# A planned order, fixed buffer places, cosines by absolute values and 128-lane convolution pairs in a two-branch sequence mixer

## The chip, the cores and the metric

The kernel runs on one core of a Trainium2 chip. The core has a matrix engine (PE, whose weight loads the profile lists apart as PEld), three engines for elementwise work (DVE, ACT, POOL), a queue engine (SP) and 16 DMA engines that all queues share. Each engine works through its own list of instructions in order and waits on semaphores where one needs what another engine or a DMA makes. The metric is the device time in microseconds of one execution; lower is better.

## The reference, cut to what matters

The input is `u`, 2048 positions by 640 channels. Two branches are mixed by a gate per position.

```python
g = _sigmoid((x * gate_w).sum(-1, keepdims=True))
# a: a long convolution per channel with a kernel of 128 damped oscillations
P = jnp.exp((A * dt[:, None])[:, :, None] * pos[None, None, :])
K = 2.0 * jnp.einsum("dn,dnl->dl", C, P).real
y = jnp.fft.irfft(jnp.fft.rfft(u_t, 2*L) * jnp.fft.rfft(K, 2*L), 2*L)[:, :, :L]   # + u * D_skip
# b: a filter in the two-dimensional spectrum
X = jnp.fft.rfft2(x) * (w_r + 1j * w_i)
b = jnp.fft.irfft2(X, s=(S, D))
return g * a + (1 - g) * b
```

Nothing of this changes.

## The kernel before, in words

The work is in five stages, with letters used from here on. Channels are cut into four chunks of 160, c = 0 to 3.

- **P** (`phase_p`): small vectors of the parameters, split into three bfloat16 parts each and written to DRAM.
- **A** (`phase_a`, first half): the first two steps of the length-4096 transform of `u`, as matrix products in float32. `stage1` (L353) multiplies blocks of 64 by 128, `stage2` (L366) blocks of 64 by 160; ACT or DVE copies each result out of PSUM (L400) and the result `u_d` goes to DRAM. Beside it the gate's sums (L435).
- **F** (`phase_a`, second half): the two-dimensional spectrum in nine groups of rows: transposes (L533), products (L487, L492), the filter on DVE (L563 to L573), the way back (L583 to L599); result `s3e_d` in DRAM.
- **K** (`phase_b`): the convolution kernel, 40 steps t in batches of five. Per step `mags` makes exponentials (L686, ACT L688), `outer` and `inner` make a phase product each (L696) and one ACT sine over 1024 columns each (L703, L715) that gives sine and cosine at once; POOL multiplies one factor (L706), DVE the other (L718, L719, L720), and PE combines them (L735) into `k_d` in DRAM.
- **C** (`phase_c`, `phase_d`): per chunk, the kernel's transform (L353, L366), the product with `u_d` on DVE (L830, L831), the sum and difference of its halves (L835, L836), the product back (L849), a copy (L851) and a write to `s3_d`; later the last step reads `s3e_d` into `t3e` (L889) and `s3_d` into `t3` (L901, each load writing every fourth lane), multiplies (L170, L928), applies the gate (L911, L931 to L934) and writes out.

Each buffer is a tile from a pool, with its own entry in the bookkeeping of waits. The order is written by generators that are merged by weights: A, then F, then the first transform of C run as one stream beside the stream of P and K (`merge((194.0, ga), (76.8, gl))`); C follows when both are done. DMAs are issued from SP, ACT and POOL.

Of the kernel before, what the change touches and what calls it, by code (L numbers as in the profile page):

```python
# [11 lines left out]
I32 = mybir.dt.int32  # L12
# [11 lines left out]
NP = 33  # L24
MAGIC = 12582912.0
# [3 lines left out]

# [13 lines left out]
def _tables():  # L51
# [34 lines left out]
    w3 = np.swapaxes(w2, 1, 2) * wk[:, None, None]  # L86
    w2[K0, 64:] = 0.0
# [28 lines left out]
    rx, ry, rm = np.zeros((128, 2, 16, 32)), np.zeros((128, 2, 8, 2, 32)), np.zeros((128, 8, 96))  # L116
    rx[[51, 115], 1] = ry[[57, 121], 1] = 1.0
    ry = ry.swapaxes(2, 3)
    for x in range(16):
        r = 64 * (x // 8) + 6 * (x % 8)  # L120
        rm[r:r + 3, x % 8, 0:64] = A_ORDER
        rm[r:r + 3, x % 8, 64:96] = 64 * j
        rm[r + 3:r + 6, x % 8, 64:96] = 1.0
        r = 3 * x if x < 10 else 3 * x + 2
        for h in (0, 64):
            rx[h + r:h + r + 3, 0, x] = j + 0.5
        rx[94 if x < 10 else 114, 0, x] = 1.0
# [39 lines left out]
def halved(nc, out, w, x):  # L167

    for i in (0, 64):
        nc.tensor.matmul(out[i:i + 64], w[:, i:i + 64], x, start=True, stop=True)  # L170


def merge(*streams):

    live = [[0.0, t, g] for t, g in streams]
    while live:
        s = min(live, key=lambda x: x[0] / x[1])
        try:
            s[0] += next(s[2])
        except StopIteration:  # L180
            live.remove(s)


def run(gen):
    for _ in gen:
        pass


def chain(*gens):
    for g in gens:  # L190
        yield from g


def body(tc, A, out):
    nc = tc.nc
    T = Ctx()
    with ExitStack() as top:
# [23 lines left out]
        T.w2 = cst.tile([128, NP, 128], F32, name="w2")  # L221
        T.gate = cst.tile([128, 2, 16], F32, name="gate")
        T.pin = None
        with ExitStack() as cctx:
            def left():
                with ExitStack() as ctx:
# [4 lines left out]
                    yield 0.0  # L231
                    yield from phase_b(tc, A, T, ctx)

            ga, gl = chain(phase_a(tc, A, T), phase_c(tc, A, T, cctx)), left()
            next(gl)
            next(ga)
            next(gl)
            while T.pin is None:
                next(ga)
# [773 lines left out]
```

## Time and profile before

| | us |
|---|---|
| median of 3 runs | 639.94 (636.74 to 640.0) |
| the profiled execution | 637.14 |
| its span in the profile | 635.3 |
| busy PE / DVE / ACT / POOL | 535.0 / 452.3 / 310.5 / 313.7 |

The page counts an engine as busy while an instruction of it runs; a matrix product counts until its modelled end. A view by line gives the instructions of one source line: busy time, mean duration in ns, and the idle time just ahead of them with what ended it. A view by stretches gives the busy time of each engine between two times. Float32 products stand twice in the profile for each one in the program (1056 against 528 at L366).

### The profile page before, as it was taken

Reading aid. Unit: us, or ns where it says so; the run is one execution under the profiler, and the core shown is the slowest. Engines: PE = TensorE matmul, PEld = TensorE weight load, DVE = VectorE, ACT = ScalarE, POOL = GpSimd, SP = SyncE. Lnnn points to the kernel's source line nnn. Section 1 sums busy time; section 2 is a strip of 40 time slices with the busy share of each in tenths; the row PEclk is TensorE's granted clock in tenths of the full one; section 3 lists DMA queues with packets and bytes.
Section 4 is the critical chain, followed back from the end, with each engine's and each line's share of the span. In section 5 each row is a group of like instructions: output and inputs, shape, how many; then the busy total and the mean of one; then the engine's idle time right before and its main releaser. Section 6 shows DMA issues by size and latency. Waiting matters only on the chain. (4 is left out here: it accounts for less than half of the span.)

```text
span 635.3 us, 17319 instructions
## 1 busy us (share of the span) xinstructions
PE 535.0 (84%) x7432; PEld 379.6 (60%) x7432; DVE 452.3 (71%) x684; ACT 310.5 (49%) x476; POOL 313.7 (49%) x345
## 2 busy tenths in 40 slices
PE   8696999979984998498998978666687999999875
PEld 6594667647653775265665646333376878876651
DVE  6991487479999798489669705242479698796965
ACT  4564634524871486445773876848531323222120
POOL 4975561563585144803292374170724346546533
PEclk9897999989996799889899999887789999999999
DMA  9776223354354134021420258200044889969767
GB/s 344 301 267 245 79 90 118 114 171 142 86 192 120 42 101 141 8 79 44 162 78 24 63 175 311 94 2 2 1 152 156 300 272 309 359 202 324 255 217 269
DMA packets 49332, 101.84 MB, mean 160 GB/s; under 512 B 4756, under 2 KB 34216, under 8 KB 47624
## 3 DMA queue, kind: packets, MB, share of 16 engines
q1 hardware_dynamic: 24888, 67.08, 30.7%
q10 hardware_dynamic: 20080, 22.52, 11.1%
q0 software_dynamic: 4288, 11.15, 5.3%
q8 instruction: 58, 0.95, 0.6%
q14 instruction: 18, 0.15, 0.1%
HBM read 60.91 MB, written 39.81 MB: 159 GB/s over the span
## 5 line engine op out<-in xcount | busy, mean ns | idle before, releaser
L706 POOL TENSOR_TENSOR y<-e,sc 128x512 f32<-128x512 f32 x80 | 106.3, 1359 | 40.8 <-ACT sc L703 40.7
L366 PE MATMUL p_s<-t,w 128*64 128x160 f32 x1056 | 94.4, 317 | 9.8 <-ACT ut L400 5.4
L366 PEld LDWEIGHTS p_s<-t,w 128*64 128x64 f32 x1056 | 76.6, 140 | 23.9 <-ACT ut L400 6.3
L735 PE MATMUL p_k<-x,y 128*32 128x64 f32 x2560 | 58.9, 239 | 35.4 <-DVE x L719 28.4
L696 PE MATMUL p_p<-tr,pxy 64*128 64x512 bf16 x480 | 77.3, 410 | 6.6 <-ACT sc L703 4.5
L735 PEld LDWEIGHTS p_k<-x,y 128*32 128x32 f32 x2560 | 46.2, 120 | 54.9 <-issue 39.9
L718 DVE SCALAR_TENSOR_TENSOR x<-e,p_p 128x512 f32<-128x512 f32 x40 | 27.3, 682 | 61.9 <-ACT p_p L715 61.8
L688 ACT ACTIVATE e<-p_e 128x1024 f32<-128x1024 f32 x80 | 62.3, 816 | 9.1 <-PE p_e L686 5.8
L715 ACT ACTIVATE p_p<-p_p 128x1024 f32<-128x1024 f32 x40 | 40.4, 1010 | 39.4 <-PE p_p L696 32.9
L354 ACT COPY t<-p_s 128x512 f32<-128x512 f32 x40 | 24.9, 621 | 66.8 <-PE p_s L353 41.2
L835 POOL TENSOR_TENSOR t<-ma 64x320 f32<-64x320 f32 x32 | 28.0, 876 | 54.4 <-DVE ma L830 52.3
L703 ACT ACTIVATE sc<-p_p 128x1024 f32<-128x1024 f32 x40 | 40.5, 1024 | 19.7 <-PE p_p L696 13.0
L720 DVE TENSOR_TENSOR x<-e,p_p 128x1024 f32<-128x1024 f32 x40 | 48.6, 1215 | 0.0
L849 PE MATMUL p_i<-t,w 128*64 128x160 f32 x528 | 43.2, 303 | 4.4 <-POOL t L836 3.4
L353 PE MATMUL p_s<-c,kt 128*64 128x128 f32 x640 | 43.2, 274 | 3.8 <-DVE mb L831 2.0
L353 PEld LDWEIGHTS p_s<-c,kt 128*64 128x64 f32 x640 | 37.9, 136 | 13.4 <-issue 8.2
L589 POOL TENSOR_TENSOR qq<-z 128x320 f32<-128x320 f32 x17 | 16.9, 992 | 57.3 <-DVE z L586 56.0
L696 PEld LDWEIGHTS <-pxy 64*128 64x128 bf16 x480 | 22.4, 98 | 38.0 <-issue 29.0
L849 PEld LDWEIGHTS p_i<-t,w 128*64 128x64 f32 x528 | 37.0, 138 | 9.3 <-POOL t L836 4.0
L353 PE MATMUL p_s<-c,u 128*64 128x128 f32 x640 | 41.5, 277 | 0.2 <-DMA u<-in_u_l 0.2
L851 ACT COPY s<-p_i 128x640 f32<-128x640 f32 x32 | 21.7, 693 | 39.5 <-PE p_i L849 34.6
L353 PEld LDWEIGHTS p_s<-c,u 128*64 128x64 f32 x640 | 35.8, 137 | 6.8 <-issue 5.0
(159 smaller groups left out, 1066.9 us busy)
## 6 DMA issues: line engine op xcount, KB each, us to landing
u_d<-ut SPq DMA_DIRECT2D x32, 320.0 KB, 3.6
us<-u_d ACTq DMA_DIRECT2D x16, 640.0 KB, 6.4
s_d<-s ACTq DMA_DIRECT2D x15, 640.0 KB, 6.3
t<-s_d SPq DMA_DIRECT2D x14, 640.0 KB, 5.6
ww<-in_w_l SPq DMA_DIRECT2D x8, 642.0 KB, 3.9
ue<-u_d SPq DMA_DIRECT2D x8, 640.0 KB, 4.3
k_d<-kt SPq DMA_DIRECT2D x4, 1280.0 KB, 4.7
kt<-k_d SPq DMA_DIRECT2D x8, 640.0 KB, 5.6
```

Source lines behind the costliest of these rows:

```text
L353: nc.tensor.matmul(p[64 * ri:64 * ri + 64, j, :], src(i + j), e1[ri], start=True, stop=True)
L366: ins = nc.tensor.matmul(p[64 * j:64 * j + 64, i, 160 * ri:160 * ri + 160], w2[:, x, 64 * ri:64 * ri + 64], t1[:, x // 2 if x < 32 else K0 ...
L688: st.exp = S.activation(ef[:, :, c:c + n], p[:, :, :n], AF.Exp)
L696: P.matmul(p[:, h, :], pars[t][1][l, v], turns[v][l, s], start=s == 0, stop=s == 2)
L703: T.trig = st.trig = S.activation(sc.rearrange("p v (h d) i -> p h v (d i)", h=2), p.rearrange("p h (v c) -> p h v c", v=2), AF.Sin, scale ...
L706: G.tensor_tensor(out=y[:, v], in0=es[t][:, :, 64:96], in1=sc[:, 1 - v], op=ALU.mult)
L715: T.trig = st.trig = S.activation(p[:, :, :], p[:, :, :], AF.Sin, scale=TWO_PI)
L718: V.scalar_tensor_tensor(out=x[:, 1, :, 32:64], in0=e[:, :, 32:64], scalar=-1.0, in1=sc[:, 0], op0=ALU.mult, op1=ALU.mult)
L720: V.tensor_tensor(out=x[:, 0].rearrange("p d (h j) -> p d h j", h=2), in0=e[:, :, 0:64].rearrange("p d (h j) -> p d h j", h=2), in1=sc[:, ...
L735: P.matmul(st.pb[32 * r:32 * r + 32, o, :], y[:, ri, 4 * qq + JR[r], :], x[:, ri, 4 * qq + JR[r], :], start=t % 2 + qq + 1 - ri == 0, stop ...
L835: (G if j else V).tensor_tensor(out=t2[0:64, o, :], in0=ma[l, :hn, 0, :], in1=ma[l, :hn, 1, :], op=ALU.subtract)
L849: T.mm = P.matmul(p[x:x + 64, i // 2, 160 * (i % 2):160 * (i % 2) + 160], T.w3[:, k0 + h + i, x:x + 64], t2[:, h + i, :], start=True, stop ...
```

## The change

Everything is rewritten around a planner; the stages keep their arithmetic save for K's cosines and C's unit.

**Places.** All of SBUF is one tile `sb` and all of PSUM one tile `ps`; buffers are column ranges of them. Stages A, F and C share one range and K and C another, one after the other.

**Order.** Each engine call is recorded as a unit with an occupation, and `order` sorts all units by a list schedule: at each step the engine with the earliest start takes the ready unit with the longest remaining path. All DMAs go to SP's queue.

**K.** `outer` and `inner` become one `phases`: one phase product gives the turns of both factors, DVE takes absolute values, and four ACT sines of 512 columns make two sines and, as sin(pi/2 - |x|), two cosines. **C.** The product's two chunks of 64 lanes stay on 128 lanes: `t2` takes sum and difference in two DVE operations, and the product back uses 64 by 64 blocks, twice as many, accumulated in pairs. The gate on `oe` moves to ACT, the last sum to one DVE operation per row.

```diff
+        sb = top.enter_context(tc.tile_pool(name="sb", bufs=1)).tile([128, WIDE], F32, name="sb")
+        ps = top.enter_context(tc.tile_pool(name="ps", bufs=1, space=PSUM)).tile([128, 8, 512], F32, name="ps")
...
+        R.emit(order(R.units, OPT))
...
+def order(units, opt):
+        u.tail = max((v.tail + (u.occ if v.eng == u.eng and u.size is None else land(u) + LAT[v.eng]) for v in follow[u]), default=land(u))
...
+                v = rank[u] - (x - s0)
+                if e == "PE" and u.mode != mode:
+                    v -= opt.get("hold", 300.0)
...
+    out.sort(key=lambda u: u.at)
+    return out
...
 # K, phases and multiplications of one step
-            T.trig = st.trig = S.activation(sc.rearrange("p v (h d) i -> p h v (d i)", h=2), p.rearrange("p h (v c) -> p h v c", v=2), AF.Sin, scale=TWO_PI)
-            T.trig = st.trig = S.activation(p[:, :, :], p[:, :, :], AF.Sin, scale=TWO_PI)
-        V.tensor_tensor(out=x[:, 0].rearrange("p d (h j) -> p d h j", h=2), in0=e[:, :, 0:64].rearrange("p d (h j) -> p d h j", h=2),
-                        in1=sc[:, 1].unsqueeze(2).broadcast_to([128, 16, 2, 32]), op=ALU.mult)
+        V.tensor_scalar(out=af.rearrange("p h v c -> p h (v c)").bitcast(I32), in0=p.bitcast(I32), scalar1=0x7FFFFFFF, scalar2=None, op0=ALU.bitwise_and)
+        for o, i, s in ((sh[:, 0], pv[:, :, 1], TWO_PI), (pv[:, :, 0], pv[:, :, 0], TWO_PI), (pv[:, :, 1], af[:, :, 0], -TWO_PI), (sh[:, 1], af[:, :, 1], -TWO_PI)):
+            u = S.activation(o, i, AF.Sin, scale=s, **({"bias": T.hpi} if s < 0 else {}))
+        for h in range(2):
+            V.tensor_tensor(out=xh[:, 0, h].rearrange("p d (y j) -> p d y j", y=2), in0=eh[:, h, :, 0:64].rearrange("p d (y j) -> p d y j", y=2),
+                            in1=cx[:, h].unsqueeze(2).broadcast_to([128, 8, 2, 32]), op=ALU.mult)
...
 # C, one unit of two pairs
-            for j in range(nj):
-                (G if j else V).tensor_tensor(out=t2[0:64, o, :], in0=ma[l, :hn, 0, :], in1=ma[l, :hn, 1, :], op=ALU.subtract)
-                (V if j else G).tensor_tensor(out=t2[64:128, o, :], in0=mb[l, :hn, 0, :], in1=mb[l, :hn, 1, :], op=ALU.add)
-                for x in (0, 64):
-                    T.mm = P.matmul(p[x:x + 64, i // 2, 160 * (i % 2):160 * (i % 2) + 160], T.w3[:, k0 + h + i, x:x + 64], t2[:, h + i, :], start=True, stop=True)
+        V.tensor_tensor(out=t2[:nl, 0, :n], in0=ma[:nl, :n, 0], in1=ma[:nl, :n, 1], op=ALU.subtract)
+        V.tensor_tensor(out=t2[:nl, 1, :n], in0=mb[:nl, :n, 0], in1=mb[:nl, :n, 1], op=ALU.add)
+            for ri in range(2):
+                for i in range(n):
+                    for j in range(nl // 64):
+                        for x in (0, 64):
+                            P.matmul(q[x:x + 64, j, 160 * i:160 * i + 160], w3[l, pr + i, ri, x:x + 64], t2[l, ri, i, :], start=ri + i == 0, stop=ri == 1 and i == n - 1)
...
 # C, the load of the last step
-                T.ld = eng.dma_start(t3s[c][y::4, :, a:a + w], src[:, :, a:a + w])
+            Y.dma_start(t3[y::4], src, reads=[("s", c, y)] + [("r33", c)] * (y == 2))
```

In the new file `stage1` is L624, `stage2` L634, the DVE copies of A L687, K's absolute values L905, its sines L908 and its multiplications L915 to L918; C's unit is L986 to L1000, the load of `u_d` L1045, the load of `t3` L1024, the last products L1015 and L1031.

How the instructions moved, at three places. The first is DVE's list in the middle of A. Before, K's multiplications (L718 to L720, into `x`) stand between A's copies:

```order
L400 COPY t_848<-p_s_1053 128x16x16x2 [waits PE_49]
L718 SCALAR_TENSOR_TENSOR x<-e,p_p 128x16x32 [waits Activation_49,Pool_49]
L719 TENSOR_TENSOR x<-e,p_p 128x16x32
L720 TENSOR_TENSOR x<-e,p_p 128x1024
L718 SCALAR_TENSOR_TENSOR x<-e,p_p 128x16x32 [waits Activation_49]
L719 TENSOR_TENSOR x<-e,p_p 128x16x32
L720 TENSOR_TENSOR x<-e,p_p 128x1024
L400 COPY t_848<-p_s_1075 128x16x16x2 [waits PE_49]
```

In the change the same place holds P's casts and A's copies alone; the first of K's operations (L905) stands behind A's last reduction:

```order
L687 COPY sb<-ps 128x320 [waits DMAHW1_49,PE_49,Activation_49]
L561 CAST sb<-sb 128x640 [waits DVE_49]
L562 TENSOR_TENSOR sb<-sb 128x640 [waits DVE_49]
L563 CAST sb<-sb 128x640 [waits DVE_49]
L564 TENSOR_TENSOR sb<-sb 128x640 [waits DVE_49]
L687 COPY sb<-ps 128x320 [waits DMAHW4_49,PE_49,Activation_49]
L687 COPY sb<-ps 128x320 [waits DMAHW5_49,PE_49,Activation_49]
```

K's DVE work has moved from A to behind A; from there to the start of C it alternates with F's.

The second place is SP's list in C, where chunk 0's `t3` is loaded from `s3_d` (named `s_d`). Before, the load waits for its source's writes and its tile:

```order
L785 DMA kt<-k_d 128x1280 [waits DMAHW4_49,PE_49]
L901 DMA t_6101<-s_d 32x5120 [waits DMAHW0_49]
L901 DMA t_6101<-s_d 32x5120 [waits DMAHW7_49]
L901 DMA t_6101<-s_d 32x5120 [waits DMAHW4_49,DMAHW3_49,DMAHW2_49]
L785 DMA kt<-k_d 128x1280 [waits PE_49]
```

In the change the first of these loads (L1024) waits for seven of the eight DMA semaphores and for DVE and ACT; the next one, a few entries later, for PE too:

```order
L1045 DMA sb<-u_d 128x1280 [waits DMAHW5_49,DVE_49]
L1000 DMA s_d<-sb 128x4x160 [waits DMAHW6_49,Activation_49]
L1024 DMA sb<-s_d 32x5120 [waits DMAHW3_49,DMAHW2_49,DMAHW4_49,DMAHW1_49,DMAHW5_49,DMAHW0_49,DMAHW7_49,DVE_49,Activation_49]
L1045 DMA sb<-u_d 128x1280 [waits DMAHW7_49,DVE_49]
L1000 DMA s_d<-sb 128x4x160 [waits Activation_49] x2
L1045 DMA sb<-u_d 64x320 [waits DVE_49]
L1045 DMA sb<-u_d 128x1280 [waits DVE_49]
L1024 DMA sb<-s_d 32x5120 [waits DMAHW1_49,DMAHW0_49,DMAHW4_49,DVE_49,DMAHW6_49,PE_49,Activation_49]
```

The load itself signals DMAHW7. Chunk 0's four loads stand apart like this, those of chunks 1 and 2 in one row of four each, chunk 3's as three and one.

The third place is DVE's list at that load. Before, a unit of C stands as two products and two half-lane operations (`t` is `t2`; POOL has the other two):

```order
L830 TENSOR_TENSOR ma<-p_s_5750,us 128x640 [waits PE_49,Pool_49]
L831 TENSOR_TENSOR mb<-p_s_5750,us 128x640 [waits Pool_49]
L835 TENSOR_TENSOR t_5722<-ma 64x2x160 [waits DVE_49]
L836 TENSOR_TENSOR t_5722<-mb 64x2x160 [waits DVE_49]
L830 TENSOR_TENSOR ma<-p_s_5780,us 128x640 [waits DMAHW2_49,PE_49,Pool_49]
```

In the change the difference L988, which reads `ma` and writes `t2`, waits for DMAHW7, the load of `t3`:

```order
L986 TENSOR_TENSOR sb<-ps,sb 128x640 [waits DMAHW7_49,PE_49,Pool_49]
L987 TENSOR_TENSOR sb<-ps,sb 128x640
L988 TENSOR_TENSOR sb<-sb 128x320 [waits DMAHW7_49,DVE_49]
L989 TENSOR_TENSOR sb<-sb 128x320 [waits DVE_49]
L986 TENSOR_TENSOR sb<-ps,sb 128x640 [waits PE_49]
```

The same wait on the load stands at the next instruction of PE, of ACT and of SP, and so again at the other loads of chunks 0 to 2.

More of the change, by code (lines that the diff above doesn't have):

```diff
@@ L1 @@
 import math
-from contextlib import ExitStack, nullcontext
+import sys
+from contextlib import ExitStack, contextmanager
 import numpy as np
@@ L164 @@
     pass
[L167 to L191, printed above, removed]
+OPT = {}
@@ L194, in body, with block @@
+@contextmanager
+def block(R, tag=None):
+    old = R.tag
+    R.tag = tag or old
+    R.open = R.unit("PE", 0.0, 165)
+    yield R.open
+    R.open = None
+    R.tag = old
 def body(tc, A, out):
@@ L220, in body @@
         T.hpi = take(1)
[L221 to L226, printed above, removed]
-                    T.bc = ctx.enter_context(tc.tile_pool(name="b_c", reuse_waits="tile", bufs=1))
-                    T.tr = T.bc.tile([128, 3840], BF16, name="tr")
-                    T.pxy = [T.bc.tile([128, 2, 5, N], BF16, name=n) for n in ("pxy0", "pxy1")]
-                    yield from phase_p(tc, A, T)
[L231 to L239, printed above, removed]
-            merge((194.0, ga), (76.8, gl))
-            phase_d(tc, A, T, cctx, out)
@@ new lines, in columns @@
+                    P.matmul(p[x:x + 32], zz[:, q, :], u[:, q, :], start=q < 4, stop=q > 15)
+            S.copy(T.lg[:, 2 * c + h, :], p)
+        for pr in range(0, 17, 2):
+            n = min(2, 17 - pr)
+            nl = 128 if pr < 16 else 64
+            ut = T.aut()
+            for i in range(n):
+                p = bank().rearrange("p (i x) -> p i x", i=1)
+                with block(R):
+                    stage2(T, p, t1, pr + i, 0)
+                src = p[:nl, 0, 0:320].rearrange("p (r d) -> p r d", r=2)
+                (V.tensor_copy if i else S.copy)(ut[:nl, i], src)
+            Y.dma_start(T.u_d[c, :nl, pr:pr + n], ut[:nl, :n], writes=[("u", c, pr + i) for i in range(n)])
@@ L526, in transposes @@
+    def transposes(src, dst, nl, back):
+        for c, (e0, e1) in enumerate(CH):
+            p = bank()
+            with block(R):
                 for x in range(4):
@@ new lines, in kgen @@
+    def kgen(t, x, y):
+        c, i = t // 10, 4 * (t % 10 - 1)
+        if t % 2 == 0:
+            st.pb = pk().rearrange("p (i a) -> p i a", i=8)
+        with block(R):
+            for qq in range(4):
+                o = 4 * (t % 2) + qq
+                for ri in (1, 0):
+                    for r in (0, 1, 2, 3):
+                        P.matmul(st.pb[32 * r:32 * r + 32, o, :], y[:, ri, 4 * qq + JR[r], :], x[:, ri, 4 * qq + JR[r], :],
+                                 start=t % 2 + qq + 1 - ri == 0, stop=t % 2 + qq - ri == 4)
+        if t % 2:
+            kt = pkt()
+            S.copy(kt, st.pb)
+            V.tensor_tensor(out=kt[:, :, 31], in0=kt[:, :, 31], in1=T.dsk[:, c, i:i + 8], op=ALU.add)
+            Y.dma_start(T.k_d[c, :, i:i + 8], kt, writes=[("k", c, i // 4), ("k", c, i // 4 + 1)])
```

1352 lines of the change are left out of this document (710 added, 642 removed).

## The prediction

> **What bounds the kernel now.** I read the page's engine line first, then the busy time by stretches, cut where the stages change, then single lines.
>
> ```profile
> PE 535.0 (84%) x7432; PEld 379.6 (60%) x7432; DVE 452.3 (71%) x684; ACT 310.5 (49%) x476; POOL 313.7 (49%) x345
> ```
> ```profile
> core 0: us, PE busy (x) PEld busy (x) DVE busy (x) ACT busy (x) POOL busy (x), PEclk, DMA share, GB/s
> 0.00:105.00 105.00, 90.25 (x1491) 70.33 (x1492) 71.93 (x103) 52.84 (x84) 64.96 (x74) 0.95 0.59 214
> 105.00:140.00 35.00, 30.63 (x504) 20.58 (x502) 20.46 (x30) 16.83 (x21) 18.38 (x19) 0.95 0.38 128
> 140.00:376.00 236.00, 202.84 (x2404) 135.26 (x2397) 189.77 (x308) 140.07 (x233) 108.18 (x126) 0.93 0.30 92
> 376.00:468.00 92.00, 65.91 (x1318) 39.09 (x1315) 35.81 (x45) 59.23 (x72) 38.87 (x37) 0.84 0.25 92
> 468.00:616.00 148.00, 132.56 (x1676) 109.78 (x1668) 125.06 (x176) 40.89 (x66) 77.57 (x85) 0.99 0.82 271
> ```
>
> PE leads with 84%, but not everywhere alike. Up to 105 us (A) and from 468 us (C) PE is busy in nearly nine tenths. From 140 to 376 (F beside K) PE has 203 and DVE 190 of 236. From 376 to 468 no engine is near full: F is over and K runs alone. How much of K is left by then shows in its combining products:
>
> ```profile
> 140.00:376.00 236.00, 27.30 (x1216) 20.81 (x1208) 0.93 0.30 92
> 376.00:468.00 92.00, 22.94 (x960) 18.60 (x960) 0.84 0.25 92
> ```
>
> 960 of 2560, three of the eight batches, in 92 us: 31 us a batch. The wait behind it is DVE's on the sine, PE and ACT handing one phase tile to and fro:
>
> ```profile
> DVE x L718 <- ACT p_p L715: 61.8, 14, 18.0
> ```
>
> C starts sharply, and the chain of waits gives its end:
>
> ```profile
> 468.16 2.04 PE L366 MATMUL p_s<-t,w 128*64 128x160 f32 x16
> ...
> 631.56 0.29 DVEq L1009
> ```
>
> So C takes 631.85 - 468.16 = 163.7 us, then 3.45 us pass to the span's 635.3 and 1.84 more to the profiled execution's 637.14. The sum has two large parts: when C starts, and how long it is.
>
> **The change, part one: up to C.** PE gives up half of the phase products, DVE takes the absolute values. The rows:
>
> ```profile
> L696 PE MATMUL p_p<-tr,pxy 64*128 64x512 bf16 x480 | 77.3, 410 | 6.6 <-ACT sc L703 4.5 <-ACT e L688 1.6 <-issue 0.5
> L718 DVE SCALAR_TENSOR_TENSOR x<-e,p_p 128x512 f32<-128x512 f32 x40 | 27.3, 682 | 61.9 <-ACT p_p L715 61.8
> L719 DVE TENSOR_TENSOR x<-e,p_p 128x512 f32<-128x512 f32 x40 | 27.2, 680 | 0.0
> L720 DVE TENSOR_TENSOR x<-e,p_p 128x1024 f32<-128x1024 f32 x40 | 48.6, 1215 | 0.0
> L400 DVE COPY ut<-p_s 128x320 f32<-128x320 f32 x38 | 17.8, 488 | 21.4 <-PE p_s L366 14.5 <-DMA u_d<-ut 4.6 <-ACT e L688 1.6
> L400 DVE COPY t<-p_s 128x512 f32<-128x512 f32 x20 | 13.8, 692 | 17.2 <-PE p_s L353 17.2
> L688 ACT ACTIVATE e<-p_e 128x512 f32<-128x512 f32 x40 | 24.2, 604 | 0.9 <-PE p_e L686 0.9
> L703 ACT ACTIVATE sc<-p_p 128x1024 f32<-128x1024 f32 x40 | 40.5, 1024 | 19.7 <-PE p_p L696 13.0 <-POOL y L706 6.1
> ```
>
> PE: 480 products become 240, 77.3 / 2 = 39 us less. DVE before C has 71.9 + 20.5 (105 to 140) + 189.8 + 35.8 = 318 us. It gains 40 absolute values over 1024 columns from PSUM, not in the trace; the nearest is L720 at 1.2 us (no less than two thirds of it, no more than two L400 copies, 1.4): +48. The 1024-column product becomes two of 512: 40 x (2 x 0.68 - 1.215) = +6. Twenty small additions come from POOL, under 0.15 us each: +3. Of the copies (17.8 + 13.8, and 1.4 in smaller ones) 32 of 320 columns stay, 16 us: -17. So 318 + 48 + 6 + 3 - 17 = 358 us. ACT goes from 80 sines of 1.02 to 160 of 0.60, +15, and takes the copies, some +17: 269 us becomes about 300, less than DVE's.
>
> A itself does not shrink. PE does 41.5 + 94.4 / 2 + 7.3 = 96 us for it from 5 us on:
>
> ```profile
> L366 PE MATMUL p_s<-t,w 128*64 128x160 f32 x1056 | 94.4, 317 | 9.8 <-ACT ut L400 5.4 <-ACT t L354 1.6 <-DVE mb L831 1.5
> L353 PE MATMUL p_s<-c,u 128*64 128x128 f32 x640 | 41.5, 277 | 0.2 <-DMA u<-in_u_l 0.2
> L435 PE MATMUL p_g<-u,z 128*32 128x64 f32 x320 | 7.3, 222 | 0.1
> ```
>
> With 4 us of waits that ends at 105. The order lists show K's DVE work behind A, so until then DVE can only do P and A's copies. Before, A's copies (L400) and K's steps (L718, one each) had by then:
>
> ```profile
> 0.00:105.00 105.00, 18.78 (x36) 0.95 0.59 214
> ...
> 0.00:105.00 105.00, 3.40 (x5) 0.95 0.59 214
> ```
>
> 71.9 - 18.8 - 5 x 2.58 = 40 for P, and 16 of copies make 56. That leaves 358 - 56 = 302 us of DVE for F beside K, more than PE has there. F beside K filled DVE to 189.8 / 236 = 80%, C to 125.06 / 148 = 85%; K evenly spread over all of F should do a little better than both, 88%: 302 / 0.88 = 343, and C starts at 448. Ends: 80% gives 483, 96% gives 420. So the stretch in which K ran alone goes away, but half of it returns, because DVE is left idle in A and carries the absolute values after it. Gain here: 468 - 448 = **20 us**.
>
> **Part two: C.** PE bounds it (132.56 of 148), so DVE's relief is worth only PE's waits for DVE and POOL, some 8 us in the idle columns of L366, L353 and here, of which I take 6:
>
> ```profile
> L849 PE MATMUL p_i<-t,w 128*64 128x160 f32 x528 | 43.2, 303 | 4.4 <-POOL t L836 3.4 <-DVE mb L831 1.0
> L487 PE MATMUL p_eo<-td,pmt 128*128 128x161 f32 x136 | 29.9, 336 | 5.6 <-DVE z L586 4.9 <-ACT pmt L536 0.6
> L492 PE MATMUL p_eo<-td,pmt 64*128 64x161 f32 x136 | 18.3, 329 | 0.0
> ```
>
> The way back has 528 entries of 128 by 64 at 43.2 / 528 = 82 ns and gets 1056 of 64 by 64. Half the lanes make an entry cheaper only if both lane halves run side by side. L492 against L487 says how far: 134 against 220 ns, 0.61. So 1056 x 82 x 0.61 = 53, **+10**; bounds 0 (full overlap) and +43 (none). C's other lines all have 128*64 shapes, so each of the 36 units now changes the array's shape twice.
>
> ```profile
> 454.20 1.72 PE L735 MATMUL p_k<-x,y 128*32 128x64 f32 x56 [0.69 <-DVE x L720]
> 455.85 1.46 PE L696 MATMUL p_p<-tr,pxy 64*128 64x512 bf16 x6
> ```
>
> Here a new shape starts 0.07 us ahead of the old one's modelled end, so I price a change at nothing. The Trainium skill (TensorEngine Tiling, Key Properties) says that a change of tiling mode drains the engine; by that rule each would uncover up to one product's 0.3 us, 72 x 0.3 = 22 us more.
>
> **The loads of `t3`.** This is the large term. In the order lists each of these loads waits for nearly all that stands ahead of it, on every engine, and the next instruction of each engine waits for the load, though it neither reads nor writes `t3`. Before, `t3` was a tile of its own and only its readers waited. Now the load, which writes every fourth lane of a range of the one tile, is taken to meet everything. Each is a wall across the core, and behind it wait the next units of C on all engines.
>
> ```profile
> L901 SPq DMA_DIRECT2D t<-s_d x16: 448/449/1314, 494.7 to 622.1; - x16
> ...
> DMA to landing us min/median/max: 3.4/5.5/7.1
> ```
> ```profile
> L830 DVE TENSOR_TENSOR ma<-p_s,us 128x640 f32<-128x640 f32 x32 | 26.3, 821 | 13.9 <-issue 9.4 <-PE p_s L366 2.7 <-POOL t L836 1.4
> L831 DVE TENSOR_TENSOR mb<-p_s,us 128x640 f32<-128x640 f32 x32 | 26.1, 815 | 0.0
> ```
> ```profile
> k_d<-kt SPq DMA_DIRECT2D x4, 1280.0 KB, 4.7
> t3e<-s3e_d SPq DMA_DIRECT2D x4, 1280.0 KB, 8.6
> ```
>
> One load lands 3.4 to 7.1 us after its issue. PE stops when its last product ahead is done, and DVE still has two operations of 0.8 us (L830, L831) before the load may go: 5.5 + 1.5 = 7 us for each of chunk 0's four (3.4 to 9.5), 28. Four in a row are 2560 KB, twice the rows of 1280 KB: 9 to 17 us, 13 each, for chunks 1 and 2: 26. Chunk 3's wall falls into the tail, where the last load was waited for before too: 6 (0 to 12). Sum **+60** (33 to 84). Nothing covers it: PE has no slack in C.
>
> C then takes 163.7 + 60 + 10 - 6 = 228. Sum: 448 + 228 + 3.45 + 1.84 = **681**. The median of before lies 2.8 above its profiled execution; I add 1: 682.
>
> **Rivals.**
> *The walls hold nobody* (10%): the loads go out so early, or so much work stands ahead of each, that nobody waits; then 448 + 163.7 + 4 + 5.3 = 621, faster. For it: a median of 5.5 us could hide behind two units. Against: the wait is in every engine's list.
> *DVE is kept full* (12%): 96% in F beside K and the walls at their lower bound, 420 + 163.7 + 33 + 4 + 5.3 = 626, faster. The place is the start of C; with walls of 33 it decides where C starts before 431. For it, a stretch of before with DVE full; against, 80% over all of F.
>
> ```profile
> 160.00:192.00 32.00, 29.34 (x262) 19.00 (x262) 31.90 (x47) 25.93 (x41) 22.50 (x20) 1.00 0.44 143
> ```
>
> *The lane halves do not overlap* (13%): +33, 714.
> *K stays a chain* (15%): F beside K at 80%, C at 483, 716. For it: each batch took 31 us alone, and the absolute value puts another 1.2 us between product and sine in every step.
> My forecast has 50%.
>
> **How the numbers follow.** Faster are the first two rivals but for a sliver, 19%; same, within 0.5% (about what a measurement can tell from no change), 4%; slower 77%. The likeliest one's own range is 650 to 712 (walls 33 to 84). The range that leaves out two in ten reaches to the faster cases and to the slower rivals: 617 to 733. By the skill's rule on drains the forecast alone would be 704.
>
> **What would show it.** Right: after the start of C, gaps of 5 to 10 us on PE, DVE and ACT at once, ended by L1024, six or so of them, 60 us in sum; DVE above 85% between 105 us and the start of C; no stretch with K alone. Wrong: no such gaps (621); C starting past 470 with DVE waiting for sines (chain); the way back at more than 60 us of PE (lane halves).

## The result and the profile after

The changed kernel takes 675.92 us (675.88 to 678.32, 4 runs) against 638.34 (636.01 to 640.0, 4 runs) for the kernel before: a ratio of 1.0601, 95% interval 1.0552 to 1.0649. It is 6% slower. The forecast was 682. Three runs that came out over 1.5% above the fastest run of the same kernel (643.86 us of the kernel before beside experiment 1, 654.96 in experiment 5, 713.81 in experiment 7) are left out of the times, ratios and views.

The page's engine line, then the busy time by stretches, cut at the end of A and at the first product of C (L634, the line of `stage2`):

```profile
PE 519.4 (77%) x7716; PEld 372.3 (55%) x7716; DVE 432.7 (64%) x764; ACT 368.9 (55%) x652; POOL 175.6 (26%) x159
```
```profile
core 0: us, PE busy (x) PEld busy (x) DVE busy (x) ACT busy (x) POOL busy (x), PEclk, DMA share, GB/s
0.00:105.00 105.00, 87.95 (x1474) 79.06 (x1476) 48.91 (x82) 52.39 (x95) 30.47 (x26) 0.93 0.65 224
105.00:427.68 322.68, 258.46 (x4009) 176.03 (x4005) 282.75 (x474) 250.27 (x428) 145.11 (x133) 0.89 0.31 101
427.68:674.10 246.42, 173.00 (x2244) 117.24 (x2240) 101.08 (x208) 66.26 (x130) 0.00 (x0) 0.82 0.55 179
...
627.00:674.10 47.10, 20.69 (x52) 3.60 (x48) 5.90 (x18) 5.75 (x17) 0.00 (x0) 0.53 0.30 105
```

PE, DVE and POOL are busy for less time than before (519.4, 432.7 and 175.6 us against 535.0, 452.3 and 313.7); only ACT, which makes more sines and more copies, has more (368.9 against 310.5) and is still at 55%. So the loss is waiting. The same cuts for the kernel before have their C row here:

```profile
468.16:635.30 167.14, 145.18 (x1732) 114.34 (x1728) 134.31 (x199) 41.58 (x67) 83.31 (x90) 0.98 0.81 267
```

C starts 40.5 us earlier (427.68 against 468.16) and lasts 79.3 longer (246.4 against 167.1). The difference, 38.8, is that of the spans (674.1 against 635.3). Where C's time went shows in its timeline: single rows of PE, ACT and DVE, with the idle time ahead of each and its releaser in brackets.

```profile
427.68 1.33 PE L634 MATMUL ps<-sb 128*64 128x160 f32 x16
...
448.28 0.48 SPq L1024 DMA_DIRECT2D sb<-s_d  x1
452.50 2.40 PE L634 MATMUL ps<-sb 128*64 128x160 f32 x16 [7.41 <-DMA sb<-s_d]
452.55 0.49 DVE L988 TENSOR_TENSOR sb<-sb 128x320 f32<-128x320 f32 x1 [7.94 <-DMA sb<-s_d]
452.56 0.70 ACT L999 COPY sb<-ps 128x640 f32<-128x640 f32 x1 [7.83 <-DMA sb<-s_d]
...
472.46 1.97 PE L624 MATMUL ps<-sb 128*64 128x128 f32 x16 [4.94 <-ACT sb L625]
483.31 2.40 PE L634 MATMUL ps<-sb 128*64 128x160 f32 x16 [4.53 <-DMA sb<-s_d]
495.85 1.63 PE L634 MATMUL ps<-sb 128*64 128x160 f32 x16 [4.00 <-DMA sb<-s_d]
546.27 1.86 PE L1015 MATMUL ps<-sb 128*64 128x480 f32 x4 [10.00 <-DMA sb<-s_d]
597.46 1.87 PE L1015 MATMUL ps<-sb 128*64 128x480 f32 x4 [13.67 <-DMA sb<-s_d]
637.06 1.87 PE L1015 MATMUL ps<-sb 128*64 128x480 f32 x4 [9.65 <-DMA sb<-s_d]
```

At 452.5 three engines that have nothing to do with `t3` start again within 0.06 us of each other, all released by the load of L1024 that SP issued at 448.28. Seven such gaps cost PE 7.41 + 4.94 + 4.53 + 4.00 + 10.00 + 13.67 + 9.65 = 54.2 us (the second is named after ACT's copy L625, which itself waited for the load). The products right after a gap are slow as well: 16 of them took 2.40 us at 452.50, and 1.33 at 427.68. The line's own view lists who waited for L1024:

```profile
who waited for it (us, times):
  PE ps L1015: 33.3, 3
  ACT sb L999: 28.0, 3
  DVE sb L986: 20.3, 2
...
  PE ps L634: 15.9, 3
...
  ACT sb L625: 10.7, 2
  PE ps L1031: 1.8, 1
```

Only the last, L1031, reads `t3`, and it waited least. The end of the program is a second loss. Its last unit's products end at 626.8, and from there 47.3 us pass to the end; before, the last of L849 ended at 617.9 and 17.4 were left. The chain of waits runs there from one product to the next:

```profile
624.44 1.03 PE ps L1031 x4
...
628.75 8.18 DMA sb<-s_d
637.06 1.88 PE ps L1015 x4
...
652.97 3.07 issue
657.06 1.89 PE ps L1031 x4
...
667.99 1.36 PE ps L1031 x4
```

From 637 us on twelve blocks of products stand in a row with their copies between each two; they share one PSUM bank. The even half (L1015) is among them; in the kernel before, only products of L928, the last half, were left by then.

### The profile page after: what moved, and what is told of

Read it like the earlier page. It is cut to its first block, busy times and chain, and to the rows that moved or that the text cites. A ratio compares the mean times of both kernels' runs of the same rounds, so it can differ in the third digit from the quotient of the medians.

```text
span 674.1 us, 18092 instructions
## 1 busy us (share of the span) xinstructions
PE 519.4 (77%) x7716; PEld 372.3 (55%) x7716; DVE 432.7 (64%) x764; ACT 368.9 (55%) x652; POOL 175.6 (26%) x159
## 4 chain that ended last, share of the span: by engine, by line
PE 37%; DVE 22%; ACT 11%; DMA 10%; issue 4%; SPq 1%; ACTq 0%; DVEq 0%
DMA sb<-s_d 6%; PE ps L634 6%; PE ps L997 5%; PE ps L624 4%; PE ps L1015 4%; DMA sb<-u_d 3%; DVE sb L918 3%; PE ps L724 3%; PE ps L900 3%; DVE sb L905 3%; ACT sb L908 3%; PE ps L933 3%; PE ps L1031 3%; PE ps L761 2%; ACT sb L889 2%
## 5 line engine op out<-in xcount | busy, mean ns | idle before, releaser
L921 POOL TENSOR_TENSOR sb<-sb 128x512 f32<-128x512 f32 x80 | 104.8, 1327 | 142.8 <-ACT sb L908 134.8
L634 PE MATMUL ps<-sb 128*64 128x160 f32 x1056 | 96.3, 325 | 29.5 <-DMA sb<-s_d 15.9
L634 PEld LDWEIGHTS ps<-sb 128*64 128x64 f32 x1056 | 79.2, 144 | 47.5 <-DMA sb<-s_d 16.7
L624 PE MATMUL ps<-sb 128*64 128x128 f32 x1280 | 88.2, 290 | 12.2 <-ACT sb L625 8.3
L624 PEld LDWEIGHTS ps<-sb 128*64 128x64 f32 x1280 | 77.5, 146 | 20.2 <-ACT sb L625 10.7
L625 ACT COPY sb<-ps 128x512 f32<-128x512 f32 x80 | 53.8, 674 | 61.2 <-PE ps L624 50.4
L889 ACT ACTIVATE sb<-ps 128x1024 f32<-128x1024 f32 (+1 forms) x80 | 63.6, 817 | 17.4 <-PE ps L888 17.1
L986 DVE TENSOR_TENSOR sb<-ps,sb 128x640 f32<-128x640 f32 (+1 forms) x36 | 28.3, 787 | 68.0 <-PE ps L634 46.2
L905 DVE TENSOR_SCALAR sb<-ps 128x1024 int32<-128x1024 int32 x40 | 48.5, 1218 | 17.3 <-PE ps L900 9.8
L1015 PE MATMUL ps<-sb 128*64 128x480 f32 (+1 forms) x96 | 29.0, 687 | 38.4 <-DMA sb<-s_d 33.3
L724 PE MATMUL ps<-sb 128*128 128x161 f32 (+3 forms) x280 | 52.8, 329 | 6.6 <-DVE sb L812 4.0
L933 PE MATMUL ps<-sb 128*32 128x64 f32 x2560 | 48.6, 231 | 9.3 <-ACT sb L937 8.7
L918 DVE TENSOR_TENSOR sb<-sb,ps 128x512 f32<-128x512 f32 x80 | 51.1, 677 | 0.0
L687 DVE COPY sb<-ps 128x320 f32<-128x320 f32 x32 | 15.6, 489 | 53.6 <-PE ps L634 39.3
```

Of the source, the lines that this page charges most:

```text
L624: T.P.matmul(p[64 * ri:64 * ri + 64, j, :], src(i + j), e1[ri], start=True, stop=True)
L625: copy(t1v[:, 4 * (q0 + i):4 * (q0 + i) + 16], p.rearrange("p q (j x y) -> p (q j) x y", j=4, y=2))
L634: T.P.matmul(p[64 * j:64 * j + 64, i, 160 * ri:160 * ri + 160], T.w2[:, x, 64 * ri:64 * ri + 64], t1[:, x // 2 if x < 32 else K0 // 2, :, ...
L724: P.matmul(p[:, 161 * i:161 * i + n], lhs(i, part), tab(i)[part][0], start=i == 0, stop=False)
L889: u = S.activation(ef[:, :, c:c + n], p[:, :, :n], AF.Exp)
L905: V.tensor_scalar(out=af.rearrange("p h v c -> p h (v c)").bitcast(I32), in0=p.bitcast(I32), scalar1=0x7FFFFFFF, scalar2=None, op0=ALU.bit ...
```

## The experiments

All times of an experiment are set against the kernel before, run on the same chip beside it; ratios have 95% intervals. The kernel before itself took about 640 us beside experiments 1, 2, 4 and the banks of 7, 638 beside 3, 5 and two of the later kernels, and 636 beside the rest. So kernels from different groups are best compared by their ratios, and a difference of a few us between them is not shown.

**1. The walls.** The load of `t3` writes neighbouring lanes, and the table has its rows in that order.

```diff
-        e1[0], e1[1], e3.reshape(4, 32, 64).swapaxes(0, 1).reshape(128, 64), e3e.reshape(128, 128), np.eye(128), one,
+        e1[0], e1[1], e3.reshape(128, 64), e3e.reshape(128, 128), np.eye(128), one,
...
-            Y.dma_start(t3[y::4], src, reads=[("s", c, y)] + [("r33", c)] * (y == 2))
+            Y.dma_start(t3[32 * y:32 * y + 32], src, reads=[("s", c, y)] + [("r33", c)] * (y == 2))
```

> The four loads of t3 write 32 neighbouring lanes each instead of every fourth lane, and the table that multiplies t3 has its rows reordered to match; the same bytes move and nothing else is edited. Theory, walls: the seven gaps ended by L1024 in the changed kernel (54 us of idle PE in sum, and products at 2.40 instead of 1.33 us a block right after them) exist only because the strided lanes are taken to overlap all other buffers. Then the gaps go, C shortens from 246 us to 180 to 192, the start of C stays at 428, and the time falls from 676 to 608 to 622, under the kernel before. Rival, the gaps only hide other work (the unit's own waits, the queue of SP): C stays over 225 and the time over 655. Middle rival, the walls go but the end of the program (627 to 674, serial products on one PSUM bank) keeps its length: 622 to 635.

Measured: 612.13 us, ratio 0.9601 (0.9527 to 0.9676). Two edited lines turn 6% slower into 4% faster. Who waited for L1024 now, and the stretches, cut at the start of C (425.08), then the first 125 us of C:

```profile
who waited for it (us, times):
  PE ps L1031: 8.1, 1
```
```profile
0.00:105.00 105.00, 88.09 (x1466) 79.30 (x1468) 48.63 (x82) 51.90 (x95) 30.19 (x26) 0.93 0.64 222
105.00:425.08 320.08, 258.34 (x4014) 177.18 (x4012) 283.10 (x474) 250.20 (x428) 145.89 (x133) 0.90 0.32 102
425.08:610.00 184.92, 157.69 (x2244) 109.55 (x2240) 100.82 (x209) 66.60 (x130) 0.00 (x0) 0.92 0.79 238
...
425.08:550.00 124.92, 124.82 (x1990) 96.85 (x1988) 82.15 (x161) 57.24 (x106) 0.00 (x0) 1.00 0.90 270
```

Only the true reader still waits. C falls from 246.4 to 184.9, by 61.5, and for its first 125 us PE is busy for 124.82 at the full clock. The theory holds: the walls exist because of the strided lanes, not because of the bytes or the queue. From the start of C to the last unit's products it is now 144.6 us (199.1 with the walls, 149.7 before the change); the end of the program is 40.3 (47.3 with the walls, 17.4 before the change). So the walls are worth 54.5 in the body and 7.0 at the end, and 22.9 of the longer end have another cause. PE does the same 2244 records in C in both kernels: it is busy 173.00 us with the walls and 157.69 without, and idle 73.4 and 27.2. Of the 61.5 us, 46.2 are idle time and 15.3 are products that ran more slowly, at a mean granted clock of 0.82 against 0.92.

All further experiments start from this kernel, called E1.

**2. The unit on 64 lanes.** Sum and difference go back to 64 lanes on DVE and POOL, the way back to 528 entries of 128 by 64.

```diff
-        V.tensor_tensor(out=t2[:nl, 0, :n], in0=ma[:nl, :n, 0], in1=ma[:nl, :n, 1], op=ALU.subtract)
-        V.tensor_tensor(out=t2[:nl, 1, :n], in0=mb[:nl, :n, 0], in1=mb[:nl, :n, 1], op=ALU.add)
+            (G if j else V).tensor_tensor(out=t2[0:64, o, :], in0=ma[l, :n, 0, :], in1=ma[l, :n, 1, :], op=ALU.subtract)
+            (V if j else G).tensor_tensor(out=t2[64:128, o, :], in0=mb[l, :n, 0, :], in1=mb[l, :n, 1, :], op=ALU.add)
...
+                    P.matmul(q[x:x + 64, i // 2, 160 * (i % 2):160 * (i % 2) + 160], w3[:, 2 * pr + i, x:x + 64], t2[:, i, :], start=True, stop=True)
```

> As the kernel with neighbouring lanes, but the unit of C does its sum and difference as in the kernel before: each on 64 lanes, half of them on POOL, and the product back has 528 entries of 128 by 64 (two records each of 82 ns in sum) instead of 1056 of 64 by 64. Theory of the prediction: the 64 by 64 form costs PE 10 us more and saves 6 us of waits for DVE and POOL, so the undone unit is 4 us faster. Rival from the trace of the changed kernel: its 64 by 64 products go at 39 to 40 ns an entry, so they cost nothing, and the undone unit is 4 to 10 us slower for the waits on POOL. Rival, neither matters once PE bounds C: within 2 us.

Measured: 612.54 us, 0.9603 (0.9512 to 0.9693), the same as E1 (612.13). The way back in E1 and here, in the view by line of C, and C's stretch here:

```profile
L997 PE MATMUL ps<-sb 64*64 64x160 f32 x1056 | 46.3, 307 | 0.0
```
```profile
L999 PE MATMUL ps<-sb 128*64 128x160 f32 x528 | 48.0, 311 | 1.3 <-POOL sb L993 0.7 <-issue 0.5
```
```profile
429.20:612.30 183.10, 153.66 (x1716) 116.58 (x1712) 121.65 (x204) 66.73 (x130) 61.81 (x68) 0.87 0.80 240
```

Twice the number of products in the same time: the two lane halves run side by side entirely. POOL's wait is 0.7 us. The times alone do not part the three cases, since their intervals reach some 6 us to either side; the traces speak for the third, with C at 183.10 us here and 184.92 in E1. The change's unit takes 21 us off DVE and 62 off POOL in C (121.65 and 61.81 here, 100.82 and 0 in E1), and no gain from that shows: in E1 PE is busy for nearly all of C's first 125 us as it is.

**3. No absolute values.** The kernel leaves out the absolute values and scales the phases by a quarter instead, so its cosines are wrong and with them K; the other work keeps its counts.

```diff
-        V.tensor_scalar(out=af.rearrange("p h v c -> p h (v c)").bitcast(I32), in0=p.bitcast(I32), scalar1=0x7FFFFFFF, scalar2=None, op0=ALU.bitwise_and)
-        for o, i, s in ((sh[:, 0], pv[:, :, 1], TWO_PI), (pv[:, :, 0], pv[:, :, 0], TWO_PI), (pv[:, :, 1], af[:, :, 0], -TWO_PI), (sh[:, 1], af[:, :, 1], -TWO_PI)):
+        for o, i, s in ((sh[:, 0], pv[:, :, 1], TWO_PI), (pv[:, :, 0], pv[:, :, 0], TWO_PI), (sh[:, 1], pv[:, :, 1], -HALF_PI), (pv[:, :, 1], pv[:, :, 1], -HALF_PI)):
```

> As the kernel with neighbouring lanes, without the 40 absolute values (L905): the two cosine activations read the phase product itself, at a quarter of the scale, so the cosines and with them K are left out of the result; PE, ACT, POOL and the other DVE work keep their counts. DVE loses 48.5 us of 283 between 105 us and the start of C, PE keeps its 258 there. Theory of the prediction, DVE's sum over its fill sets the start of C: with neighbouring lanes C starts at 425, and 48.5 / 0.9 = 54 us less would put it at 371, but PE at 93% then ends at 382, so 380 to 395 and a time of 565 to 582. Rival, PE and its waits bound the stretch already: C at 415 to 425 and 602 to 612. Rival, the absolute value's place in the chain from product to sine counts and not DVE's sum: the same time as in the first case, but with DVE's fill unchanged near 88%.

Measured: 589.52 us, 0.9257 (0.9205 to 0.9309). C starts at 403.29:

```profile
105.00:403.29 298.29, 254.61 (x4009) 175.41 (x4008) 241.62 (x434) 249.02 (x430) 146.99 (x133) 0.90 0.35 110
```

C starts 21.8 us earlier, between the 30 to 45 of the first case and the 0 to 10 of the second: DVE lost 41.5 us there (283.10 in E1), and its fill, the share of the stretch in which it is busy, went from 88% to 81%. DVE's sum counts, but for about half; PE at 85% and ACT at 83% are close behind. No case that was written down holds alone.

**4. Cosines as before.** Two phase products a step and two sines of 1024 columns, no absolute values.

```diff
-        V.tensor_scalar(out=af.rearrange("p h v c -> p h (v c)").bitcast(I32), in0=p.bitcast(I32), scalar1=0x7FFFFFFF, scalar2=None, op0=ALU.bitwise_and)
-        for o, i, s in ((sh[:, 0], pv[:, :, 1], TWO_PI), (pv[:, :, 0], pv[:, :, 0], TWO_PI), (pv[:, :, 1], af[:, :, 0], -TWO_PI), (sh[:, 1], af[:, :, 1], -TWO_PI)):
+        p = turned(z, 1)
+        u = S.activation(sc.rearrange("p v (h d) i -> p h v (d i)", h=2), p.rearrange("p h (v c) -> p h v c", v=2), AF.Sin, scale=TWO_PI)
...
+        p = turned(z, 0)
+        u = S.activation(p, p, AF.Sin, scale=TWO_PI)
```

> As the kernel with neighbouring lanes, but K makes its cosines as in the kernel before: two phase products a step instead of one and one sine of 1024 columns each, no absolute values. DVE loses 48.5 us (40 x 1.218) and about 2.5 us of split products, PE gains about 39 us, ACT goes back from 160 sines of 0.6 to 80 of 1.02. In the changed kernel DVE is busy 283 of the 323 us from 105 us to the start of C (88%), PE 258 (80%). Theory of the prediction, DVE bounds that stretch: C starts earlier, but PE then has 298 of work for it and becomes the bound at once, so the gain is at most 10 us and the time is that of neighbouring lanes -10 to +5. Rival, PE bounds the stretch: +20 to +39. Rival, DVE alone bounds it: -25 to -45.

Measured: 606.50 us, 0.9514 (0.9427 to 0.9600), 5.6 under E1, which the intervals do not part from no difference. The time lies in the range of the first case, and C starts at 414.2, 10.8 earlier:

```profile
105.00:414.24 309.24, 270.62 (x4283) 181.25 (x4281) 257.75 (x391) 228.38 (x348) 148.28 (x132) 0.97 0.35 112
```

The reason given for it is not shown. PE was to have 298 us of work in the stretch and to bound it; it has 270.62, which is 87.5%, at a granted clock of 0.97 against 0.90 in E1. And K is not done when C starts: its last DVE operation ends at 423.4, against 425.1 in E1.

**5. K first.** The order prefers K's and P's units to all others.

```diff
-OPT = {}
+OPT = {"bias": {"K": 100000.0, "P": 100000.0}}
```

> As the kernel with neighbouring lanes, but the order prefers K's and P's units to all others that could start, A's included. In the changed kernel DVE is busy 49 of the first 105 us. Theory of the prediction, the start of C is late because DVE idles in A and carries its work later: with K's steps in A, some 20 us of DVE work are done there and C starts 15 to 25 us earlier, time 587 to 600. Rival, A is bound by PE (88 of 105), K's products push A's back by as much, and F starts later: within 5 us of 612. Rival, K runs ahead and F is then left alone, which has less work for DVE: later start of C, 615 to 640.

Measured: 645.90 us, 1.0157 (1.0093 to 1.0220), by the ratios some 35 us slower than E1. DVE did 68.67 us of work in A instead of 48.63, as wanted, and C still started 36.8 later:

```profile
0.00:105.00 105.00, 79.73 (x1414) 64.71 (x1416) 68.67 (x97) 61.45 (x105) 45.49 (x36) 0.95 0.53 186
105.00:440.00 335.00, 267.26 (x3886) 182.67 (x3882) 263.18 (x459) 233.49 (x405) 127.06 (x123) 0.90 0.31 98
440.00:461.88 21.88, 15.49 (x185) 11.32 (x187) 0.00 (x0) 7.56 (x15) 0.08 (x1) 0.92 0.65 232
```

The last row is almost only the first transform of C; DVE is still. The third case holds in kind, and the loss is larger than its 615 to 640: K's last DVE operation ends at 336.0 and F's at 439.5, so F runs alone for 103 us. In E1 F's ends first, at 384.9, and K's at 425.1.

**6. DVE and POOL laid side by side.** The planner's rule that holds DVE's operations with two SBUF inputs and POOL's apart is switched off.

```diff
-                    u.lock = len(sbuf) > 1 or bool(two)
+                    u.lock = False
...
-                    u.lock = True
+                    u.lock = False
```

> As the kernel with neighbouring lanes; only the planner's rule that DVE's operations with two inputs from SBUF and POOL's operations are not laid beside each other is switched off, so the same operations stand in another order. Before the change the same operation on 320 columns (L590) took 480 to 3073 ns, median 1036; in the changed kernel (L816) 473 to 811, median 485. Theory: DVE's operations slow down when POOL works beside them, and the rule is why DVE's work before C came out 26 us under my 358. Then L816's median rises towards 1 us, DVE's busy time before C rises from 332 by 10 to 26 us, and the time by 3 to 20. Rival, the buffers' places or the fewer POOL operations did it: DVE's busy time within 3 us, time within 4 us or faster.

Measured: 617.32 us, 0.9721 (0.9636 to 0.9807), 5.2 above E1, with intervals that meet; C starts at 432.4. DVE's work before C is 337.0 against 331.7 (48.63 + 283.10 in E1; the changed kernel has 48.91 + 282.75, the same sum):

```profile
0.00:432.38 432.38, 348.76 (x5477) 258.52 (x5479) 337.01 (x556) 302.36 (x522) 178.91 (x159) 0.90 0.39 130
```

One operation's durations (min/median/max) before the change, after it, and here:

```profile
L590 DVE TENSOR_TENSOR qq<-z x17: 480/1036/3073, 170.7 to 371.3; 128x320 f32<-128x320 f32 x17
```
```profile
L816 DVE TENSOR_TENSOR sb<-sb x17: 473/485/811, 166.0 to 387.4; 128x320 f32<-128x320 f32 x17
```
```profile
L816 DVE TENSOR_TENSOR sb<-sb x17: 474/487/1047, 170.3 to 391.9; 128x320 f32<-128x320 f32 x17
```

The median did not move, and 5 of the missing 26 us came back, less than the first case asked for and more than the second. The rule does a fifth of it.

The traces show more than this one line. L590 alone and L590 beside POOL, before the change:

```profile
205.80 0.48 DVE L590 TENSOR_TENSOR qq<-z 128x320 f32<-128x320 f32 x1
...
209.79 0.93 POOL L589 TENSOR_TENSOR qq<-z 128x320 f32<-128x320 f32 x1 [4.68 <-DVE z L586]
210.02 1.04 DVE L590 TENSOR_TENSOR qq<-z 128x320 f32<-128x320 f32 x1
```

F has 143 DVE operations that read SBUF alone. Before the change 36 of them took over 0.1 us longer than the shortest one of their shape, and in the changed kernel 28; each of these had an operation of POOL beside it. The time above the shortest comes to 32.5 us for those with POOL beside them and 0.7 for the others before the change, and to 18.0 and 0.9 in the changed kernel. F's other 104 DVE operations read PSUM too, and none was over 0.03 us longer, with POOL beside it or not. So what F's DVE work lost is time beside POOL. With the rule off it is 22.4 us, against 18.4 in E1; why the rest of the difference to the kernel before stays away, by the other order or by POOL's fewer operations, no run separates.

**7. The end.** Two PSUM banks for chunk 3's last products; another place for its `t3`; both, with the cosines as before.

```diff
+        if c == 3:
+            bl.banks = [7, 0]
...
         t3 = t3p()
+        if c == 3:
+            b = t1p.bases[0]
+            t3 = R.sb[:, b:b + 5120].rearrange("p (x a d) -> p x a d", x=2, a=16)
```

> As the kernel with neighbouring lanes, and chunk 3's last products (L1015, L1031) take turns between two PSUM banks instead of one. Theory, chain on one bank: in the changed kernel the last products and their copies run one after the other from 637 to 653 and from 654 to 670, a product of 1.9 us and then about 1 us of copies, six times each; with two banks the copies go beside the products, 5 to 12 us faster than with neighbouring lanes alone. Rival, the products of the end are bound by the load or by the low clock: within 2 us of it.

> As the kernel with neighbouring lanes; chunk 3's t3 lies in the columns of the t1 buffer that chunk 2 has done with. With neighbouring lanes alone 40.3 us pass from the end of the last unit's products (569.7) to the end, against 17.4 in the kernel before (617.9 to 635.3), which is the part of the end that is left when the walls are gone. Theory, the one t3 buffer, which chunk 2's last products hold until 569, puts off three of chunk 3's four loads: the end gets 8 to 12 us shorter, time 600 to 605. Rival, the one PSUM bank is what makes the end long: within 3 us of 612.

> Three edits together: neighbouring lanes for t3, K's cosines as in the kernel before, and two PSUM banks for chunk 3's last products. With neighbouring lanes alone 612, the cosines alone took 6 us of it and the banks alone 1 to 5; if they add, 600 to 605; if the end of the program is bound by the landing of the last loads of t3, 604 to 608.

> The three edits together (neighbouring lanes, K's cosines as before, two PSUM banks at the end), and chunk 3's t3 lies in the columns of a t1 buffer that chunk 2 has done with, instead of in the one t3 buffer that chunk 2's last products hold. With the three edits PE stood 10.7 us at the end for four loads issued together at 566 to 569 us. Theory, the buffer holds those loads: three of them go out earlier, only the last one of 640 KB is waited for, and the time falls by 5 to 9 us, to 592 to 597. Rival, the DMA queues are the limit at the end (busy 0.79 to 0.95): within 3 us of 601.6.

| kernel | us | ratio (95%) |
|---|---|---|
| E1 | 612.13 | 0.9601 (0.9527 to 0.9676) |
| E1, two banks | 611.13 | 0.9573 (0.9489 to 0.9657) |
| E1, `t3` elsewhere | 608.74 | 0.9568 (0.9480 to 0.9657) |
| E1, cosines as before | 606.50 | 0.9514 (0.9427 to 0.9600) |
| the same, two banks | 601.62 | 0.9438 (0.9383 to 0.9492) |
| the same, two banks, `t3` elsewhere | 596.75 | 0.9386 (0.9346 to 0.9426) |

By the times the banks alone and the place alone are worth nothing that can be told, against 5 to 12 and 8 to 12 expected. Where both are done with the cosines, it is by the ratios some 8 us less than the cosines alone, and the two intervals just no longer meet. The views of the load, PE's row of each, show what the banks change: for E1 with the banks, for the cosines with the banks, and for the same with `t3` elsewhere too:

```profile
  PE ps L1031: 10.1, 2
```
```profile
  PE ps L1044: 10.7, 1
```
```profile
  PE ps L1047: 5.1, 2
```

With the banks the products stop waiting for each other and wait a little longer for the load (8.1 us in E1), and with `t3` elsewhere too that wait halves. From its first product of C to the end a profiled execution takes 184.9 us in E1 and 179.6 with the banks; with the cosines 185.9, with the banks too 180.8, and with `t3` elsewhere too 177.4. So in the traces the banks are worth 5 us with either cosines and the place 3 more. The end, from the last unit's products on, is 38.4 us with cosines and banks and 29.5 (565.2 to 594.7) with the place too, but there those products also end later, by 5.4 us counted from C's start. That the two waits cover each other is not shown.

**8. Two more orders.** Last products preferred by 40 us, on the kernel with two banks and the cosines as before; and K by 15 us, on the one with `t3` elsewhere too.

```diff
+        R.tag = "L"
         oe = even(c)
         last(c, oe)
...
-OPT = {}
+OPT = {"bias": {"L": 40000.0}}
```

> As the three edits together, and the last products of every chunk (L1010 to L1035 in the changed kernel) are preferred by the order by 40 us of remaining path. With neighbouring lanes the last products of chunk 2 run at 540 to 570 us, beside chunk 3's units, and hold the one t3 buffer, so that chunk 3's first three loads go out at 570 only and share the queues with the last write of s3_d. Theory, the end is bound by that: chunk 3's loads come earlier and the end is 5 to 12 us shorter, 590 to 600. Rival, the preferred products take PE's time from the units and only the order changes: within 3 us of the three edits. Rival, a load that waits at the head of SP's queue holds the loads of u_d behind it: 5 to 20 us slower.

```diff
-OPT = {}
+OPT = {"bias": {"K": 15000.0, "P": 15000.0}}
```

> As the one before, and the order prefers K's and P's units by 15 us of remaining path. Preferring them outright (by 100 us) made K end early, left F alone on the engines, and cost 36 us. Theory, before C the end is set by how evenly K's DVE work is spread over F's PE work, and K's last products still run when C starts: a little earlier is better, 3 to 10 us faster than the one before. Rival, any push of K ahead leaves F alone for longer: 3 to 15 us slower. Rival, the push is too small to change the order: within 3 us.

The first: 605.92 us, 0.9523 (0.9470 to 0.9575), 4.3 above the kernel it starts from, with intervals that meet; no gain, and PE waits 15.1 us for the loads of `t3` instead of 10.7. The second: 592.21 us, 0.9322 (0.9275 to 0.9368), 4.5 under its base, the size that was forecast, but with intervals that meet. Not as told: C's first product came later (420.4 against 417.3), but no product of K was left beside it and C was shorter, 170.6 against 177.4. It is the fastest kernel found that computes all of K, 6.8% under the one before.

## Why the prediction was right, and where its steps were not

The forecast of 682 was 6 above the measured 675.9, with the sign and the main cause right. By its own steps, on the spans (679.5 forecast, 674.1 measured):

| step | forecast | measured | |
|---|---|---|---|
| C starts | 448 | 427.7 | -20.3 |
| walls, the one at the end included | +60 | +61.5 (E1 against the changed kernel) | +1.5 |
| way back and waits for DVE in C's units | +10 - 6 | -5.1 (144.6 against 149.7) | -9.1 |
| the rest of the end | 0 | +22.9 (40.3 against 17.4) | +22.9 |

These four sum to -5.0; the spans differ by -5.4, the rest is rounding. The last two rows share some work: in E1 the even products of chunk 3 (571 to 582 us) lie in the end, and in the kernel before they lay among the units. So the sum was right partly by luck, because errors cancelled: C began 20 us too early for it, and the end was 23 us too long.

**The walls** were right in mechanism and place, and in size as a sum. The prediction had 28 for chunk 0's four, 13 each for chunks 1 and 2, and 6 for the end. The gaps were 20.9, 10.00, 13.67 and 9.65, so chunk 0's came out a quarter cheaper and the end's dearer. (The lower bounds given add up to 31.6 and not 33, which changes nothing.) "Nobody waits" (10%) is refuted by the timeline, and E1 shows the cause. By the difference between the kernels they cost 7 more than PE's gaps. The prediction had no term for the slower products behind a gap, which are the 15.3 us of the 61.5 in experiment 1; that 60 came so near is partly luck.

**The start of C.** The step that failed is the term "318 + 48 + 6 + 3 - 17 = 358 us" of DVE work. The edits themselves were priced rightly; the absolute values took

```profile
L905 DVE TENSOR_SCALAR sb<-ps 128x1024 int32<-128x1024 int32 x40 | 48.5, 1218 | 17.3 <-PE ps L900 9.8 <-ACT sb L908 4.5 <-PE ps L888 2.6
```

48.5 against 48. Summed over the view by line, K's operations took 58.5 us more than before (57 forecast) and A's 18.1 less (17 forecast). What was wrong was to carry the 318 over: the same operations of F and P took less (F's 164.6 became 150.7 and P's 43.1 became 35.1), and DVE had 331.7 to do. In F that is time lost beside POOL (experiment 6), which the prediction took for the operations' own; P's 8 us were not traced to a cause.

The fill was forecast at 88% and was 282.75 / 322.68 = 87.6%. But it is the mean of two parts that the prediction did not tell apart, cut where F's last DVE operation ends:

```profile
105.00:387.90 282.90, 226.31 (x3268) 153.70 (x3263) 261.96 (x441) 220.88 (x381) 131.70 (x123) 0.90 0.30 94
387.90:427.68 39.78, 32.15 (x741) 22.33 (x742) 20.78 (x34) 29.39 (x48) 13.41 (x11) 0.88 0.40 146
```

Beside F DVE is 93% busy. Then K's last steps run for 40 us beside C's first transform and what is left of F on PE, with DVE at 52%. So K was not spread evenly over F, a stretch without F stayed, and that the mean hit 88% is luck. Nor is the fill a constant to divide by: with 41.5 us less DVE work it fell to 81% (experiment 3). The reason given, that half the gain returns "because DVE is left idle in A", is not borne out: the order that filled A with K's work cost some 35 us (experiment 5), since F was then left alone. "DVE kept full" asked for 96% and a start before 431: the start came there, but by less work and not by more fill, and the walls were 61 and not 33. "K stays a chain" is refuted, with C at 428 and not 483.

**The lane halves** cost nothing. The ratio of 0.61 taken from L492 against L487 did not carry over; those products have 128 columns of weights and these 64, and whether that is the reason no run shows. The rival (+33) is refuted more clearly. The rule weighed there, that a change of tiling mode drains the engine (the Trainium skill, TensorEngine Tiling, Key Properties), would have put 22 us on C's 72 changes; in E1 PE is busy 124.82 of 124.92 us across most of them, and the kernel whose units do not change the mode (experiment 2) is no faster. No drain of that size shows in this case; one of a few us in all could hide in the scatter of the times.

**The end** was the term "6 (0 to 12)". It priced the last load alone. It missed that the even products and the last ones share one bank, and that `t3` has one buffer that chunk 2's last products hold until 570.4 in E1, so that chunk 3's loads go out together. Undone together they shorten C by 8 us in the traces (experiment 7); what makes the rest of the end long stays open.

## What to carry to other kernels

When buffers become ranges of one large tile, whoever keeps the waits must still see that two of them do not meet: look in the order lists for an instruction on which every engine waits, and price it as a barrier, by its time to landing plus what the engines must finish first. A load that writes neighbouring lanes instead of strided ones was here worth 64 us with the same bytes, because nothing but its reader waits for it any more.

A sum of one engine's work over a fill is a good first number and a poor lever: taking work away moved the end by half of it, and moving the work earlier by force made it worse. Before durations are carried over to another order, see what ran beside them. At the end of a program look at all waits on one buffer or bank together: when the products no longer waited for their bank, they waited longer for the load.

## What the runs showed of the hardware beyond the forecast

- After a gap of some microseconds PE's products run at about half speed for a while: 16 of L634 took 2.40 us behind a gap of 7.41 and 1.33 otherwise, and four products of L1031 took 1.89 at 657.06, with PE mostly waiting, and 1.03 at 624.44. The granted clock was 0.53 from 627 us to the end. The Trainium skill (TensorE: Matmul & The Clock Gate, What's actually happening) has PE's clock at half speed after an idle window of about 3.4 us until it has been busy for about as long, and the trace agrees in kind, with factors of 1.8. So a wait of some microseconds costs more than its length.
- Products of 64 by 64 on the two lane halves overlap wholly: 1056 in 46.3 us against 528 of 128 by 64 in 48.0.
- The same DVE operation on two SBUF inputs took between 480 and 3073 ns before the change and 473 to 811 after it. The Trainium skill (SBUF — State Buffer, Who interferes with whom) has DVE and POOL share a port pair that only one of them holds at a time. The traces agree: in F all operations that were slowed by over 0.1 us had POOL beside them and read SBUF alone, 32.5 us in sum before and 18.0 after, and 104 operations with an input from PSUM were not slowed. Keeping the two apart in the planned order was worth 5 us of DVE's time.
